# Routed experts in three passes, two of them among the steps of a delta rule

## The chip, the cores and the metric

The kernel runs on one core of a Trainium2 chip. The metric is the time of one execution in microseconds on the device. The engines of the core are PE (matrix products), ACT (scalar engine), DVE (vector engine), POOL (GpSimd) and SP, which only issues transfers. Each runs its own queue of instructions in order and waits on semaphores of the others.

## What is computed

A delta rule with 4 x 8 heads, 768 tokens and head size 48 gives 3072 rows of 384 numbers. A router then sends each row to two of eight experts, and each expert is a two-layer network of 384 to 1024 to 384 numbers. All is float32.

```python
for t in range(S):
    y[:, :, t] = einsum('bhd,bhde->bhe', q[:, :, t], state)
    v_old = einsum('bhde,bhd->bhe', state, k_n[:, :, t])
    state = state + beta[t] * einsum('bhd,bhe->bhde', k_n[:, :, t], v[:, :, t] - v_old)
...
noisy = x @ w_gate + log1p(exp(x @ w_noise)) * noise     # x: 3072 rows of 384
top2, top2_w = two largest of noisy, softmax of the two
for e in range(8):
    rows = tokens with e among their two
    out[rows] += top2_w * (relu(x[rows] @ w1[e]) @ w2[e])
```

A token has two rows, one for each of its experts. Of 6144 rows an expert gets between 711 and 807.

## The kernel before

**Two stages.** The first stage computes the delta rule and the routing, the second the experts.

**First stage.** The 768 tokens are cut into 12 chunks of 64, and two chunks make a step: there are six steps (s = 0 to 5, called steps 1 to 6 in the text), each with four units (two chunks by two pairs of the batch). For each step: `products` transposes k and multiplies it with itself (L433, L449), and copies the diagonal blocks into `gd`; `invert` inverts 32 x 32 triangles on DVE (L495 takes `gd` into `t`, L538 scales by `low_d`, which POOL makes in L531, then thirty columns in L546 and L550, L562 scales, L570 and L576 transpose back to `tb` and `tt`); `within` multiplies q with k (L433, L449, L641); `join` puts the 32-blocks together to 64-blocks `w64` (L594, L606); `recur` carries the state from chunk to chunk (L449 with `st`, L679, L689, L707, L719, and L732 on POOL, which makes `wide`); `answer` gives the rows y and the router's logits (L751, L762, L771, L776); `route` picks the two experts of each token, counts the rows that each expert has so far (`before`; L882 to L888 on PE) and writes each row, with its token number and weights, into the expert's part of the array `rows_x` in DRAM, by eight indirect writes from POOL (L319, called spreads).

**Who sets the order.** In the first stage no loop order is kept. Every piece is a job of the class `Jobs` with an engine, an assumed cost, what it reads and writes, and sometimes a due time (multiples of PACE = 42). `order` places the jobs by these costs, engine by engine, the earliest due first among those that could start at about the same time, and PSUM is given out to the jobs as halves of four pairs of banks. The jobs are then emitted in that order, and each engine's queue is in that order from then on. q, k, v and other operands lie in rings of buffers; a ring's size says how far ahead of its use a load or a product can be made:

```python
NK, NT_, NW = 3 * US, 3 * US - NU, US + NU        # US = 4 units of a step, NU = 2
NQ, N_U, N_ST = 2 * NU, 2 * NU + 1, 3
```

`kps` (k) has NK = 12 slots, `kTs` (its transposes) and `ats` NT_ = 10, `w64s` 6, `us` 5, the states 3.

**Transfers ahead.** While the first steps run, SP also writes empty rows into `rows_x` (eight transfers), clears `out` (one), and loads the weights of the first expert into `w_even`.

**Second stage.** When all rows are written, the eight experts follow one after the other, each with 832 rows: six tiles of 128 and one of 64. For each: the rows are loaded (L1119, L1122), then the weights of the next expert (L285, L286, two buffers of both weights, `w_even` and `w_odd`), the sums so far of these tokens are gathered from `out` (L1084, seven indirect reads on POOL), the rows are transposed (L1023, L1027), the first layer is made in two halves of 416 columns (L1033, ReLU in L1037), the second layer tile by tile (L1058; the tile of 64 in L1044), each result is added to the gathered sum with its weight (L1062, L1049) and scattered back to `out` (L1093). The gathers of an expert wait for the scatters of the one before, since a token has rows of two experts. If an expert had more than 832 rows, a block behind the end would do the rest; with these inputs it is not entered.

The buffers of the second stage lie where the first stage had its own, so they can be written only when that pool's users are done.

Of the kernel before, what the change touches and what calls it, by code (L numbers as in the profile page):

```python
# [21 lines left out]
ROWS = TILES * 128 + MORE  # L22
ROW = 384 + 4
HALF = ROWS // 2

# [3 lines left out]
class Bank:  # L29
# [5 lines left out]
    def __init__(self, size, ahead=False):  # L35
        self.size, self.ahead, self.tile, self.users = size, ahead, None, []


class Jobs:

# [12 lines left out]
    def add(self, engine, cost, emit, reads=(), writes=(), opens=None, uses=None, closes=None,  # L53
            lands=0.0, due=None):
        job = SimpleNamespace(
            engine=engine, cost=cost, emit=emit, opens=opens, closes=closes, lands=lands,
            due=1e9 if due is None else due, after=set(), number=len(self.jobs),
        )
        bank = opens or uses or closes
        if bank:  # L60

            if bank.users:
                job.after.add(bank.users[0])
            if closes:
                job.after.update(bank.users)
            if uses and engine == self.PE:
                job.after.update(bank.users)
            bank.users.append(job.number)
        for key in reads:
            job.after.update(self.wrote.get(key, ()))  # L70
        for key in writes:
            job.after.update(self.wrote.get(key, ()))
            job.after.update(self.read.get(key, ()))
        for key in reads:
            self.read.setdefault(key, []).append(job.number)
        for key in writes:
            self.wrote[key], self.read[key] = [job.number], []
        job.after.discard(job.number)
        self.jobs.append(job)

    def order(self):
        jobs = self.jobs
        for job in reversed(jobs):
            for i in job.after:
                jobs[i].due = min(jobs[i].due, job.due - job.cost - self.SIGNAL)
        waits = [len(job.after) for job in jobs]
# [12 lines left out]
        def place(size, ahead):  # L99

            best = None
            for i, pair in enumerate(halves[: self.AHEAD] if ahead else halves):
                if size == 2:
                    if None not in pair:
                        best = min(best or (1e9,), (max(pair), 0, i, 0))
                    continue
                for z in range(2):
                    if pair[z] is not None:

                        best = min(best or (1e9,), (pair[z], pair[1 - z] is not None, i, z))  # L110
            return best

        done = []
        while len(done) < len(jobs):
            first = {(x, y): place(x, y) for x in (1, 2) for y in (False, True)}
            best = None
            for engine in self.ENGINES:
                at = []
                for i in could[engine]:
                    start = max(free[engine], ready[i])  # L120
                    if jobs[i].opens:
                        room = first[jobs[i].opens.size, jobs[i].opens.ahead]
                        if room is None:
                            continue
                        start = max(start, room[0])
                    at.append((start, jobs[i].due, i))
                if at:
                    soon = min(at)[0] + self.PATIENCE
                    pick = min((x for x in at if x[0] <= soon), key=lambda x: x[1:])
                    best = min(best or (1e9,), pick)  # L130
# [4 lines left out]
            if job.opens:  # L135
                _, _, x, z = first[job.opens.size, job.opens.ahead]
                job.opens.at = x, z
                for y in range(z, z + job.opens.size):
                    halves[x][y] = None
                pair = self.pairs[x]  # L140
                job.opens.tile = pair if job.opens.size == 2 else pair[:, z]
# [17 lines left out]
    AHEAD = 3  # L159
# [6 lines left out]
def kernel(  # L166
# [12 lines left out]
):  # L179

# [101 lines left out]
    def load_weights(pool, e):  # L282
        w1e = pool.tile([128, KT, F], FP32, name="w1e")
        w2e = pool.tile([128, FT, DM], FP32, name="w2e")
        nc.sync.dma_start(out=w1e, in_=w1r[e])  # L285
        nc.sync.dma_start(out=w2e, in_=w2r[e])  # L286
        return w1e, w2e
# [42 lines left out]

    def deltanet(ictx):
# [5 lines left out]
        PE, ACT, DVE, POOL, SP = Jobs.ENGINES  # L337

# [22 lines left out]
        NK, NT_, NW = 3 * US, 3 * US - NU, US + NU  # L361

        NQ, N_U, N_ST = 2 * NU, 2 * NU + 1, 3
        kps = ring([128, H, DP], "kp", NK, lambda t: [t[:, :, D:DP]])
        qps = ring([128, H, DP], "qp", NQ, lambda t: [t[:, :, D:DP]], nc.vector)
# [42 lines left out]
        def load(n, name):  # L408
            c, u = divmod(n, NU)
            src, t, size = {"k": (k, kps, NK), "q": (q, qps, NQ), "v": (v, vs, NQ)}[name]  # L410
# [15 lines left out]
        def turned(n, name, src, size, to, to_size):  # L426

            p = Bank(1, True)
# [26 lines left out]
        def products(n):  # L455
# [6 lines left out]
            p = Bank(2, True)  # L462
# [117 lines left out]
        def join(n):  # L580
# [5 lines left out]
            p = Bank(1)  # L586
# [41 lines left out]
        def within(n):  # L628

            turned(n, "q", qps, NQ, qTs, NQ)  # L630
            p = Bank(2, True)
# [16 lines left out]
        def recur(n):  # L648
# [18 lines left out]
            if c:  # L667
                p_b = Bank(2)
# [15 lines left out]
            p_u = Bank(1)  # L684
# [16 lines left out]
            p_s = Bank(2)  # L701
# [37 lines left out]
        def answer(n):  # L739
# [4 lines left out]
            p_y, p_xt = Bank(1), Bank(1)  # L744
# [76 lines left out]
        def route(s):  # L821
# [8 lines left out]
            p = Bank(1)  # L830
# [115 lines left out]
            for i in range(US):  # L946
                for to in slot:
# [3 lines left out]
                        lands=2.5, due=(s + 1 + (s + 1 < NS)) * PACE,  # L951
                    )

# [5 lines left out]
        held = {}  # L959
        for e in range(E):  # L960
# [6 lines left out]
        jobs.add(  # L967
            SP, 2.0, lambda: held.update(w=load_weights(w_even, 0)), due=3 * PACE
        )

# [8 lines left out]
        jobs.add(SP, 0.7, clear_out, due=4 * PACE)  # L979
        for s in range(NS):  # L980
# [15 lines left out]
            route(s)  # L996
        with tc.manual_schedule(
# [6 lines left out]
        return held["w"]  # L1004

    with ExitStack() as ictx:
        weights = deltanet(ictx)
# [31 lines left out]
    def second_half(w2e, hT, gate, got):  # L1039

        p_o = ps([128, DM], "p_o")
        halves = [slice(lo, lo + MORE) for lo in (0, 64)]
        for fo in range(FT):
            nc.tensor.matmul(  # L1044
                p_o[halves[fo % 2]], hT[:, fo, ROWS - MORE : ROWS], w2e[:, fo],
# [20 lines left out]
    def gates_of(xr, e, gate):  # L1066

        nc.vector.scalar_tensor_tensor(
            out=gate, in0=xr[:, :, DM + 3], scalar=float(e - E), in1=xr[:, :, DM + 2],
            op0=ALU.is_equal, op1=ALU.mult,  # L1070
        )
        nc.vector.tensor_tensor(out=gate, in0=gate, in1=xr[:, :, DM + 1], op=ALU.add)

    def ordered(d, group, earlier):

        tc.declare_no_dep(d, group=group, reason="no token has two rows of an expert")
        tc.add_to_no_dep_group(group, d)
        for i in earlier:
            tc.add_manual_dep(d, i.name, SYNC, reason="sums so far of the same tokens")
        return d  # L1080

    def gather(got, index, group, earlier):
        return ordered(
            nc.gpsimd.indirect_dma_start(  # L1084
                out=got, out_offset=None, in_=out,
                in_offset=bass.IndirectOffsetOnAxis(ap=index, axis=0),
                bounds_check=N - 1, oob_is_err=False,
            ).ins, group, earlier,
        )

    def scatter(got, index, group, earlier):
        return ordered(
            nc.gpsimd.indirect_dma_start(  # L1093
                out=out, out_offset=bass.IndirectOffsetOnAxis(ap=index, axis=0), in_=got,
                in_offset=None, bounds_check=N - 1, oob_is_err=False,
            ).ins, group, earlier,
        )

# [10 lines left out]
    sums = [moe.tile([128, TILES + 1, DM], FP32, name=f"sums{i}", bufs=1) for i in range(2)]  # L1109
    for got in sums:  # L1110
        nc.gpsimd.memset(got, 0.0)
    rows_in = [128] * TILES + [MORE]
    for e in range(E):
        w1e, w2e = weights
        rows = slice(e * N, e * N + TILES * 128)
        more = slice(rows.stop, rows.stop + MORE)
        xr = moe.tile([128, TILES + 1, ROW], FP32, name="xr")
        loads = [
            nc.sync.dma_start(  # L1119
                out=xr[:, 0:TILES], in_=rows_x[rows].rearrange("(t p) d -> p t d", p=128)  # L1120
            ).ins,
            nc.sync.dma_start(out=xr[0:MORE, TILES], in_=rows_x[more]).ins,  # L1122
# [4 lines left out]
        if e + 1 < E:  # L1127
            weights = load_weights(w_odd if e % 2 == 0 else w_even, e + 1)
        index = moe.tile([128, TILES + 1], I32, name="index")
        gate = moe.tile([128, TILES + 1], FP32, name="gate")  # L1130
        for p, t in ((128, slice(0, TILES)), (MORE, slice(TILES, TILES + 1))):
# [4 lines left out]
            gather(got[0:p, i], index[0:p, i : i + 1], f"out{e}", added)  # L1136
# [3 lines left out]
        xe = moe.tile([128, KT, ROWS], FP32, name="xe")  # L1140
        for i, p in enumerate(rows_in):
            transposed(xr, xe, i, p)
        hT = moe.tile([128, FT, ROWS], FP32, name="hT", bufs=1)
        for h0 in range(0, ROWS, HALF):
            first(w1e, xe, hT, slice(h0, h0 + HALF))
        for i, p in enumerate(rows_in):
            if p < 128:
                second_half(w2e, hT, gate[:, i : i + 1], got[:, i])
            else:
                second(w2e, hT, i, gate[:, i : i + 1], got[:, i])  # L1150
            added.append(
                scatter(got[0:p, i], index[0:p, i : i + 1], f"out{e}", gathers if i == 0 else [])
# [79 lines left out]
```

## Time and profile before

| | |
|---|---|
| time, median of 3 runs | 1005.68 us (1004.72 to 1006.64) |
| time of the profiled execution | 1009.23 us |
| its span, first to last instruction | 1007.5 us |
| PE busy | 854.3 us (85%), 8670 matmul records |
| DVE, ACT, POOL busy | 341.5, 250.0, 235.8 us |
| moved by DMA | 95.55 MB, 95 GB/s over the span |
| mean granted TensorE clock | 0.862 of full speed |

A float32 matmul leaves two records in the profile, a transpose one. Records overlap in the array, so the time that one adds is the group's busy time over its count, and its own duration is longer. "Idle before" in a group or a timeline is how long the engine had nothing to run ahead of the instruction, and what ended that. A slice of the page is a fortieth of the span, 25.2 us. The granted clock is the share of full speed that the chip allowed to TensorE.

### The profile page before, as it was taken

Reading aid. Unit: us, or ns where it says so; the run is one execution under the profiler, and the core shown is the slowest. Engines: PE = TensorE matmul, PEld = TensorE weight load, DVE = VectorE, ACT = ScalarE, POOL = GpSimd, SP = SyncE. Lnnn points to the kernel's source line nnn. Section 1 sums busy time; section 2 is a strip of 40 time slices with the busy share of each in tenths; the row PEclk is TensorE's granted clock in tenths of the full one; section 3 lists DMA queues with packets and bytes.
Section 4 is the critical chain, followed back from the end, with each engine's and each line's share of the span. In section 5 each row is a group of like instructions: output and inputs, shape, how many; then the busy total and the mean of one; then the engine's idle time right before and its main releaser. Section 6 shows DMA issues by size and latency. Waiting matters only on the chain. (4 is left out here: it accounts for less than half of the span.)

```text
span 1007.5 us, 20278 instructions
## 1 busy us (share of the span) xinstructions
PE 854.3 (85%) x8670; PEld 581.5 (58%) x8670; DVE 341.5 (34%) x941; ACT 250.0 (25%) x613; POOL 235.8 (23%) x280
## 2 busy tenths in 40 slices
PE   4368778676968767199999999999999999999995
PEld 3267677576857656155555555555555555555552
DVE  6957768496785832210200200201201102002001
ACT  4354635545464243011020020020110110210200
POOL 3120341504315130520121121211301302202111
PEclk7757667596875858599999999999999999999998
DMA  4699631413213010462232412412511521301100
GB/s 79 122 361 374 149 82 26 112 27 89 58 25 96 12 65 3 153 233 74 71 123 79 141 53 87 163 29 88 177 62 40 167 71 54 97 16 42 41 25 28
DMA packets 119765, 95.55 MB, mean 95 GB/s; under 512 B 84558, under 2 KB 109676, under 8 KB 119664
## 3 DMA queue, kind: packets, MB, share of 16 engines
q1 hardware_dynamic: 107568, 65.34, 22.5%
q0 software_dynamic: 9984, 28.42, 8.3%
q8 instruction: 70, 1.15, 0.5%
q10 hardware_dynamic: 2112, 0.39, 0.2%
q14 instruction: 31, 0.25, 0.1%
HBM read 60.10 MB, written 35.60 MB: 95 GB/s over the span
## 5 line engine op out<-in xcount | busy, mean ns | idle before, releaser
L1033 PE MATMUL p_h<-xe,w1e 128*128 128x416 f32 x768 | 271.0, 514 | 6.3 <-DVE xe L1027 6.3
L1058 PE MATMUL p_o<-w2e,hT 128*128 128x384 f32 x768 | 249.0, 486 | 0.0
L1033 PEld LDWEIGHTS p_h<-xe,w1e 128*128 128x128 f32 x768 | 145.6, 190 | 127.5 <-issue 119.9
L1058 PEld LDWEIGHTS p_o<-w2e,hT 128*128 128x128 f32 x768 | 145.9, 190 | 102.2 <-issue 2.5
L1037 ACT ACTIVATE hT<-p_h 128x416 f32<-128x416 f32 x128 | 66.2, 517 | 491.5 <-PE p_h L1033 474.3
L1062 DVE SCALAR_TENSOR_TENSOR sums<-p_o,gate,sums 128x384 f32<-128x384 f32 x48 | 29.7, 618 | 451.9 <-PE p_o L1058 451.9
L1093 POOL DMA_INDIRECT out_dram<-sums,index x56 | 55.1, 983 | 406.3 <-DVE sums L1062 383.9
L1084 POOL DMA_INDIRECT sums<-out_dram,index x56 | 56.0, 999 | 55.5 <-issue 39.7
L546 DVE TENSOR_TENSOR part<-t 128x30 f32<-128x30 f32 (+9 forms) x180 | 63.9, 355 | 5.3
L550 DVE TENSOR_TENSOR t<-t,part 128x30 f32<-128x30 f32 (+9 forms) x180 | 63.1, 350 | 6.2
L319 POOL DMA_INDIRECT rows_x<-y,slot x48 | 47.9, 999 | 56.6 <-DVE r_count L910 29.5
L689 PE MATMUL pair<-v,w 64*64 64x48 f32 x768 | 43.0, 270 | 13.8 <-issue 13.2
L689 PEld LDWEIGHTS pair<-v,w 64*64 64x64 f32 x768 | 39.1, 184 | 16.8 <-issue 16.2
L732 POOL COPY wide<-st 64x384 f32<-64x384 f32 x44 | 29.0, 659 | 63.1 <-DVE st L719 57.4
L620 ACT COPY w<-tt 32x256 f32<-32x256 f32 x96 | 38.6, 402 | 1.8
L1023 PE MATMUL p_xt<-ident,xr 128*128 128x128 f32 (+1 forms) x168 | 22.2, 288 | 17.6 <-DMA xr<-rows_x 17.6
L449 PE MATMUL pair<-qT,kT 64*64 64x64 f32 x768 | 21.3, 269 | 17.9 <-DVE qk L641 9.0
L478 ACT COPY gd<-pair 32x256 f32<-32x256 f32 x88 | 31.9, 362 | 17.2 <-PE pair L449 14.2
L558 POOL MEMSET t<- 128x32 f32 x6 | 0.9, 156 | 139.5 <-DVE t L550 139.5
L1023 PEld LDWEIGHTS p_xt<-ident,xr 128*128 128x128 f32 (+1 forms) x168 | 19.5, 151 | 23.4 <-issue 23.4
L606 PE MATMUL pair<-w,x 32*32 32x32 f32 x768 | 25.2, 229 | 8.8 <-ACT x L601 3.3
L449 PE MATMUL pair<-kT 64*64 64x64 f32 x768 | 20.4, 273 | 13.4 <-ACT kT L438 7.6
(134 smaller groups left out, 830.5 us busy)
## 6 DMA issues: line engine op xcount, KB each, us to landing
w1e<-in_moe_w_dram SPq DMA_DIRECT2D x8, 1536.0 KB
w2e<-in_moe_w_dram SPq DMA_DIRECT2D x8, 1536.0 KB
rows_x<-empty SPq DMA_DIRECT2D x8, 1358.0 KB
xr<-rows_x SPq DMA_DIRECT2D x8, 1164.0 KB
v<-in_v_dram SPq DMA_DIRECT2D x48, 96.0 KB
qp<-in_q_dram SPq DMA_DIRECT2D x48, 96.0 KB
out_dram<-empty SPq DMA_DIRECT2D x1, 4608.0 KB
kp<-in_k_dram SPq DMA_DIRECT2D x44, 96.0 KB
```

Of the source, the lines that this page charges most:

```text
L319: d = nc.gpsimd.indirect_dma_start(out=rows_x, out_offset=bass.IndirectOffsetOnAxis(ap=slot, axis=0), in_=rows, in_offset=None,).ins
L449: nc.tensor.matmul(out[rows_of[b], z, j], lhsT[rows_of[z], j, rows_of[b]], rhs(rows_of[z], j, b), start=(j == 0), stop=(j == NP - 1), skip ...
L546: v_.tensor_tensor(out=part, in0=t_inv[:, j + 1 :, j, None].to_broadcast(shape), in1=t_inv[:, None, j, 0:j].to_broadcast(shape), op=ALU.mult,)
L550: v_.tensor_tensor(out=t_inv[:, j + 1 :, 0:j], in0=t_inv[:, j + 1 :, 0:j], in1=part, op=ALU.add)
L620: lambda rows=rows, cols=cols: nc.scalar.copy(w64[rows, :, cols], tt[rows]),
L689: nc.tensor.matmul(per_head(p_u)[b, h], w64[b, h], v_n[b, h], start=(h == 0), stop=(h == H - 1), skip_group_check=True,)
L1023: nc.tensor.transpose(p_xt[:, do, 0:rows], xr[0:rows, i, do * 128 : (do + 1) * 128], ident[0:rows, 0:rows],)
L1033: nc.tensor.matmul(p_h, w1e[:, do, fo * 128 : (fo + 1) * 128], xe[:, do, cols], start=(do == 0), stop=(do == KT - 1),)
L1037: nc.scalar.activation(hT[:, fo, cols], p_h, ACTF.Relu)
L1058: nc.tensor.matmul(p_o, hT[:, fo, i * 128 : (i + 1) * 128], w2e[:, fo], start=(fo == 0), stop=(fo == FT - 1),)
L1084: nc.gpsimd.indirect_dma_start(out=got, out_offset=None, in_=out, in_offset=bass.IndirectOffsetOnAxis(ap=index, axis=0), bounds_check=N - ...
L1093: nc.gpsimd.indirect_dma_start(out=out, out_offset=bass.IndirectOffsetOnAxis(ap=index, axis=0), in_=got, in_offset=None, bounds_check=N - ...
```

## The change

The experts are done in three passes. The first pass takes the first two tiles (256 rows) of each expert once step 2 is routed, the second the next two once step 4 is routed, and the third the remaining 2 x 128 + 64 rows at the end. To make the cut fit, an expert that has fewer than 256 (or 512) rows by then has its count raised to that, so that its later rows begin behind the cut (`cut`); the rows left out stay empty ones. By these inputs no expert ends above 807 rows.

The sixteen turns of the first two passes (`work_on`: one expert, two tiles) are jobs of the planner of the first stage, marked `late`: among jobs that could start at about the same time a late one comes behind all others, and late ones follow each other by turn. They use PSUM pair 0 alone, which from step 3 on the delta rule leaves to them, one buffer for each of the two weights, which are loaded once in each pass, and two buffers for rows, gathered sums and transposed rows. To make room, rings of the delta rule become smaller: `kps` 8 slots, `kTs` and `ats` 8, `w64s` 5, q 3, `us` 4, the states 2. In the last pass the first layer of an expert is made in one piece of 320 columns. Clearing `out` is due earlier.

```diff
+CUT = 2
+PASSES = 2
+LAST = TILES - PASSES * CUT
...
+        for job in jobs:
+            job.key = (0, job.due) if job.late is None else (1, job.late)
...
-                    at.append((start, jobs[i].due, i))
+                    at.append((start, jobs[i].key, i))
...
+        def bank(s, size, ahead=False):
+            among = (0, 1, 2, 3) if s < 2 else (1, 2, 3)
+            return Bank(size, among[:-1] if ahead else among)
...
-        NK, NT_, NW = 3 * US, 3 * US - NU, US + NU
-        NQ, N_U, N_ST = 2 * NU, 2 * NU + 1, 3
+        NK, NT_, NW = 2 * US, 2 * US, US + 1
+        NQ, NQ_IN, N_U, N_ST = 2 * NU, 3, 2 * NU, 2
...
+        def cut(rows):
+            p = Bank(1, (1, 2, 3))
+            missing = sb([1, E], f"missing{rows}")
+            def skip():
+                nc.vector.tensor_scalar(
+                    out=missing, in0=p.tile[0:1, 0:E], scalar1=-1.0, scalar2=float(rows),
+                    op0=ALU.mult, op1=ALU.add,
+                )
+                nc.vector.scalar_tensor_tensor(
+                    out=before[0:1], in0=missing, scalar=0.0, in1=before[0:1],
+                    op0=ALU.max, op1=ALU.add,
+                )
+            jobs.add(PE, 0.4, lambda: nc.tensor.matmul(p.tile[:, 0:E], ones, before),
+                     reads=["before"], opens=p)
+            jobs.add(DVE, 0.4, skip, writes=["before"], closes=p)
+
+        def work_on(x, e, steps):
+            turn = x * E + e
+            z = turn % 2
+            r0 = e * N + x * CUT * 128
+            xr, got, xe, index, gate = xrs(z), gots(z), xes(z), indices[z], gates(z)
+            tiles = range(CUT)
...
+            jobs.add(SP, 0.7, lambda: nc.sync.dma_start(out=w1e, in_=w1r[e]),
+                     writes=["w1"], lands=8.0, late=turn - 0.7)
+            jobs.add(SP, 0.7, lambda: nc.sync.dma_start(out=w2e, in_=w2r[e]),
+                     writes=["w2"], lands=8.0, late=turn - 0.4)
+            jobs.add(
+                SP, 0.7, load_rows,
+                reads=[("rows", s, i, y) for s in steps for i in range(US) for y in (0, 1)],
+                writes=[("xr", z)], lands=2.5, late=turn - 0.9,
+            )
+            jobs.add(DVE, 0.6, of_rows, reads=[("xr", z)], writes=[("gate", z)], late=turn - 0.8)
+            for i in tiles:
+                jobs.add(
+                    POOL, 1.3,
+                    lambda i=i: added_by.setdefault((turn, "got"), []).append(
+                        gather(got[:, i], index[:, i : i + 1], f"out{turn}", added_by[turn - 1])
+                    ),
+                    reads=[("gate", z), *(("out", turn - 1, j) for j in tiles)],
+                    writes=[("got", z, i)], lands=2.5, late=turn - 0.1,
+                )
...
+            for fo in range(FT):
+                p = Bank(1, (0,))
+                def hidden(fo=fo, p=p):
+                    for do in range(KT):
+                        nc.tensor.matmul(
+                            p.tile[:, 0 : CUT * 128], w1e[:, do, fo * 128 : (fo + 1) * 128],
+                            xe[:, do], start=(do == 0), stop=(do == KT - 1),
+                        )
+                jobs.add(
+                    PE, 1.3, hidden, reads=["w1", *(("xe", z, i) for i in tiles)], opens=p,
+                    late=turn,
+                )
...
+            for i in tiles:
+                p = Bank(1, (0,))
+                for f0 in range(0, FT, 2):
+                    def back(i=i, p=p, f0=f0):
+                        for fo in range(f0, f0 + 2):
+                            nc.tensor.matmul(
+                                p.tile[:, 0:DM], hT[:, fo, i * 128 : (i + 1) * 128],
+                                w2e[:, fo], start=(fo == 0), stop=(fo == FT - 1),
+                                skip_group_check=True,
+                            )
+                    jobs.add(
+                        PE, 1.3, back,
+                        reads=["w2", *(("hT", fo) for fo in range(FT))], late=turn + 0.5,
+                        **({"uses": p} if f0 else {"opens": p}),
+                    )
+                jobs.add(
+                    DVE, 0.65,
+                    lambda i=i, p=p: nc.vector.scalar_tensor_tensor(
+                        out=got[:, i], in0=p.tile[:, 0:DM], scalar=gate[:, i : i + 1],
+                        in1=got[:, i], op0=ALU.mult, op1=ALU.add,
+                    ),
+                    reads=[("gate", z)], writes=[("got", z, i)], closes=p, late=turn + 0.5,
+                )
...
-        jobs.add(
-            SP, 2.0, lambda: held.update(w=load_weights(w_even, 0)), due=3 * PACE
-        )
...
             route(s)
+            if s % 2 and s + 1 < NS:
+                x = s // 2
+                cut((x + 1) * CUT * 128)
+                for e in range(E):
+                    work_on(x, e, range(2 * x, 2 * x + 2))
...
+    both = room_for_weights(w_odd), weights_even
     for e in range(E):
-        w1e, w2e = weights
-        rows = slice(e * N, e * N + TILES * 128)
+        w1e, w2e = both[e % 2]
+        nc.sync.dma_start(out=w1e, in_=w1r[e])
+        r0 = e * N + PASSES * CUT * 128
+        rows = slice(r0, r0 + LAST * 128)
...
-        for h0 in range(0, ROWS, HALF):
-            first(w1e, xe, hT, slice(h0, h0 + HALF))
+        first(w1e, xe, hT, slice(0, LAST * 128 + MORE))
```

## The prediction

> **What bounds the kernel now.** I read the span in slices first, then the busy times of three stretches, then the costliest groups, then the timelines of the two places where the stretches meet the change. The slices show two kernels in one:
>
> ```profile
> PE   4368778676968767199999999999999999999995
> DVE  6957768496785832210200200201201102002001
> PEclk7757667596875858599999999999999999999998
> ```
>
> The first 16 slices are the delta rule, in which no engine is full and the granted TensorE clock moves between half and full. From slice 17 on PE is full at full clock: the experts. The same by stretches (PE, PEld, DVE, ACT, POOL busy, then granted clock, DMA share, GB/s):
>
> ```profile
> 176.00:405.00 229.00, 170.44 (x4178) 152.85 (x4171) 143.34 (x404) 102.42 (x274) 68.95 (x82) 0.72 0.21 54
> 405.00:431.00 26.00, 6.51 (x30) 5.93 (x30) 5.92 (x25) 0.00 (x0) 15.36 (x14) 0.50 0.55 190
> 431.00:997.00 566.00, 557.70 (x1813) 315.47 (x1811) 66.09 (x157) 66.18 (x128) 107.57 (x110) 1.00 0.26 85
> ```
>
> So PE idles 59 us in steps 3 to 6 of the delta rule, then nearly all of a 24.6 us hand-over (406.5, end of the last routing matmul, to 431.05), and 8 us in the experts. What an expert matmul costs is in the groups, as busy time over count, since matmuls overlap: 271.0/768 = 0.353 us for a record of 416 columns (0.848 ns a column) and 249.0/768 = 0.324 us for 384. Each float32 matmul leaves two records.
>
> ```profile
> L1033 PE MATMUL p_h<-xe,w1e 128*128 128x416 f32 x768 | 271.0, 514 | 6.3 <-DVE xe L1027 6.3
> L1058 PE MATMUL p_o<-w2e,hT 128*128 128x384 f32 x768 | 249.0, 486 | 0.0
> ```
>
> What paces the delta rule is the inversion on DVE, one per step, with one buffer t:
>
> ```profile
> 237.13 1.93 DVE L495 STREAM_TRANSPOSE t<-gd 128x1024 f32<-128x1024 f32 x1
> 253.87 0.56 DVE L719 TENSOR_TENSOR st<-pair,st 128x384 f32<-128x384 f32 x1 [7.92 <-PE pair L707]
> 256.44 1.22 DVE L538 TENSOR_TENSOR t<-t,low_d 128x1024 f32<-128x1024 f32 x1
> 289.83 1.22 DVE L562 TENSOR_TENSOR low_d<-t,d 128x1024 f32<-128x1024 f32 x1
> 296.61 1.87 DVE L495 STREAM_TRANSPOSE t<-gd 128x1024 f32<-128x1024 f32 x1
> ```
>
> It begins (L495), waits for the state update in the queue ahead of it (L719, 7.92 us for PE), multiplies (L538), runs its columns (to L562) and the next begins at once: 59.5 us from L495 to L495. The L562 instants of steps 2 to 6 are 106.6, 166.4, 229.9, 289.8 and 350.5; the last routing matmul starts at 404.1. PE pieces between a routing and L538 are on this chain, pieces between L538 and the next routing lie beside DVE's columns. The hand-over:
>
> ```profile
> 417.02 0.96 POOL L319 DMA_INDIRECT rows_x<-y,slot  x1 [0.30 <-issue]
> 420.18 0.37 SPq L1119 DMA_DIRECT2D xr<-rows_x  x1
> 426.53 4.58 PE L1023 MATMUL p_xt<-ident,xr 128*128 128x128 f32 x21 [17.65 <-DMA xr<-rows_x]
> 431.05 34.51 PE L1033 MATMUL p_h<-xe,w1e 128*128 128x416 f32 x96
> ```
>
> Eight spreads at 1.27 us, landing, the load of the rows, transposes; PE has nothing else to do.
>
> **The change: what moves.** A turn (two tiles of an expert) has 24 first-layer matmuls of 256 columns (48 x 256 x 0.848 ns = 10.4 us), 16 second-layer ones (32 x 0.324 = 10.4) and 6 transposes (0.126 each, from 16.1 us for 129). In the built program's order on PE only 72 of the 384 first-layer matmuls, 40 of the 256 second-layer ones and 24 of the 96 transposes stand ahead of the last routing: 31.3 + 25.9 + 3.0 = 60.2 us. Three turns of 16 are among the delta rule; 13 first layers and 13.5 second layers follow it in one block. The total of columns is the old one (256 + 256 + 320 = 832), as is the count of gathers and scatters (56 each). New are 32 weight loads of 1.5 MB.
>
> **Sum behind the delta rule.** Routing matmuls 2.4. The block: 13 x 10.4 + 13.5 x 10.4 = 275.6, and 13 turn boundaries. There the last ReLU (between 0.362, a copy of 256 columns, and 0.517, the ReLU of 416), the second transpose and the copy of the first one stand in a row ahead of the second layer, because the block has only two half pairs of PSUM: about 1.15 us a turn with its 0.76 of transposes, 15 in all (bounds 0.76 and 2.5: 10 to 33). Weights have one buffer: the next first-layer load may start when the first layer is done and has 11.5 us, the other has 10.4. The stretch 424 to 442 moved 339 to 376 GB/s, so 1.57 MB is 4.2 to 4.7 us and 2.3 to land (927.2 to 929.3, a scatter's): 7 us, hidden with 3 to spare; with the cover gone, each us late costs 13. Scatter, landing, two gathers (0.92 + 2.2 + 2 x 1.3 + 2.2, rows at 926 to 932) end 8 us into a turn whose sums are wanted at 16: hidden. Block: 291.
>
> Then a second hand-over: the first tail load waits for all readers of the delta pool, that is for the last scatter: sum 0.9, scatter 1.3, landing 2.3, then a weight load and the rows 6.5 and a transpose and copy 2: 13 us (bounds 0, were nothing waited for, and the 24.6 of now). The tail: 48 x 320 x 0.848 = 13.0, 32 x 0.324 = 10.4, half tile 2.7 (496.45 to 499.18), nine transposes and their copy 2.4: 28.5 an expert, 228. From the last matmul to the end 10.5, as now (997.0 to 1007.5).
>
> Sum: 404.1 + 2.4 + 291 + 13 + 228 + 10.5 = 949, plus what the delta rule stretches, x. The old hand-over is gone because the block fills it, and the 60.2 us left the back.
>
> **What the delta rule stretches.** Rings shrink (k 12 to 8 slots, its transposes 10 to 8, PSUM pairs 4 to 3 from step 3 on), and the order changes with them: the products of the next step (L449), on which L495 waits, no longer stand ahead of the routing but within the join. I place L495 by the PE rows ahead of it, then 10 us to L538 (transpose 1.9, squares 0.4, ACT root 2.5, lengths 2, low_d on POOL 2.34), then 32 us to L562: columns 127.0/6 = 21.2 and their gaps 2, L538 itself 1.2, routing 5.4, rest 2 (it is 33.4 to 43 now, with waits that then lie ahead of L538).
> Step 2: L495 behind the state update at 124 (now 112.5), L562 at 169.7: +3.
> Step 3: DVE takes indices and gates of the first two turns ahead of the state update and L495, and PE their transposes ahead of L707. They wait for the eight spreads (now issued to 190.1, then to about 188.5, and 2.2 to land) and a row load (3): L495 at 200 (now 175.4). POOL holds low_d behind two gathers; queued with it are wide and v, and the answers of the step wait for these. L562 at 241: +11.
> Step 4: the second-layer pieces (10.4) and five first-layer ones (6.5) stand between the routing and L707; the two sums on DVE stand ahead of L495, a scatter, its landing and two gathers on POOL ahead of low_d. L495 about 25 us behind the routing, now 8; the 7.92 wait is gone in exchange. L562 at 303: +13.
> Step 5: 10.4 us of second layer, but half of it while DVE makes tb and tt: L562 at 361, +10.5. Step 6: pieces of 3.9 and 5.2 lie in the waits for tb and for the routing's logits: last routing at +12.
> On SP three weight loads stand ahead of q and v loads of steps 5 and 6; 4.2 to 4.7 us each, 0 to 9 on the path: 3. So x = 15. Bounds: 60, nothing hidden; -5, if dense PE work raises the clock: rows of 32 records take 1.06 to 1.14 at 0.50 clock and 0.69 at full, a dozen ahead of each L538, 5 us a step.
>
> In 250 to 260 us the granted clock is 0.50 though PE reads 8.84 of 10 busy, so a piece may well start at half clock; I price the pieces at full clock, because they make the stretch denser, and leave the rest to the bound of 60. [...]
>
> **Total.** 949 + 15 = 964 of span. The profiled execution of now has a span of 1007.5 and a time of 1009.2, 3.5 above the median of the runs, so I expect 962.
>
> **Rivals.** (a) The chain through DVE loses all pieces and the reordering: L495 a further 10 us late in four steps, on top of 60: 949 + 100 = 1049 at worst, 1020 in the middle. For it: two queues, DVE and POOL, now wait for expert data ahead of the inversion. Against: 59 us of PE idleness, and L538 waits for PE already. It decides from 59 us, some 15 a step. Slower, 0.13. (b) The block is bound by its loads: late by 4 us a turn, 962 + 52 = 1014; for it the single buffers, against it 4.1 MB a turn is 190 GB/s where 376 was moved. 0.07. (c) The clock goes up among the pieces and x is -5 or less: 935 to 942. For it the 0.72 clock, against it DVE's columns, which no clock shortens. 0.09. (d) The parts cancel: 0.03.
>
> **Numbers.** Forecast 962, chance 0.68, itself from 942 to 1000. With (c) faster is 0.77 and some more from (a) and (b) when they cost half: 0.79; within 0.2% (about what these runs can tell from no change) 0.03; slower 0.18. The range 938 to 1003 leaves out a fifth.
>
> **What would show it.** L562 instants near 170, 241, 303, 361; the last routing near 419; a block of 13 turns of 22 us with PE full; 13 us without PE near 715; eight experts of 28.5. Wrong would be turns over 24 us (loads), L562 intervals over 75 us (a), or under 58 throughout (c).

## The result, and the profile after

The changed kernel is slower: 1166.29 us in the median (1161.95 to 1166.67, four runs) against 1006.16, a ratio of 1.158 (95% interval 1.154 to 1.162). The prediction was 962. The span of the profiled execution is 1164.2 us, 200 more than the 964 that the sum gave. The span in slices, first PE's busy tenths, then the granted clock:

```profile
PE   4574693698786887977777777877775799999995
PEclk7566585599897995999999999999999899999998
```

Slices 18 to 30 are the block of turns behind the last routing. There the clock is full and yet PE is busy only seven or eight tenths of the time. In the kernel before, everything behind the hand-over read nine. The block takes 404 us (488.9 to 893.3) where 291 were forecast. Two turns' edge in PE's timeline (start, duration, engine, line; in brackets the idle time before and what ended it), then the ReLUs of the same moment on ACT:

```profile
616.97 1.46 PE L1093 MATMUL pair<-xe,w1e 128*128 128x256 f32 x6
619.14 1.56 PE L1093 MATMUL pair<-xe,w1e 128*128 128x256 f32 x6 [0.71 <-DVE got L1128]
621.22 1.56 PE L1093 MATMUL pair<-xe,w1e 128*128 128x256 f32 x6 [0.52 <-ACT hT L1104]
623.32 1.56 PE L1093 MATMUL pair<-xe,w1e 128*128 128x256 f32 x6 [0.53 <-ACT hT L1104]
```

```profile
620.78 0.38 ACT L1104 ACTIVATE hT<-pair 128x256 f32<-128x256 f32 x1 [14.04 <-PE pair L1093]
622.88 0.38 ACT L1104 ACTIVATE hT<-pair 128x256 f32<-128x256 f32 x1 [1.71 <-PE pair L1093]
```

The first piece of the turn ends at 618.43, but its ReLU starts only at 620.78, 0.08 us after the second piece has ended (619.14 + 1.56); and the third piece starts 0.06 us after that ReLU. PE and ACT take turns although two banks are there: a piece every 2.10 us, where its six records of 256 columns need 1.30. A turn lasts 30.86 us (602.94 to 633.80, from transpose to transpose), not 22. PE's three longest sums of waits in the block, by what it waited for (total us, times, longest):

```profile
PE pair L1093 <- ACT hT L1104: 40.7, 77, 0.5
PE pair L1077 <- ACT xe L1082: 10.8, 12, 0.9
PE pair L1115 <- DVE got L1128: 10.0, 13, 0.8
```

No transfer is among them, nor among the six smaller sums (24.4 us together, at most 0.8 each time): the weight loads are hidden, as forecast.

The other loss lies in the delta rule. The last L938 (the count of earlier rows, L888 before) runs at 488.5 instead of 405.9, 82.7 us late, where 15 were forecast. DVE's timeline shows the form of it:

```profile
190.88 1.21 DVE L612 TENSOR_TENSOR low_d<-t,d 128x1024 f32<-128x1024 f32 x1
236.38 1.98 DVE L545 STREAM_TRANSPOSE t<-gd 128x1024 f32<-128x1024 f32 x1 [1.66 <-ACT gd L528]
244.73 1.26 DVE L588 TENSOR_TENSOR t<-t,low_d 128x1024 f32<-128x1024 f32 x1
275.86 1.22 DVE L612 TENSOR_TENSOR low_d<-t,d 128x1024 f32<-128x1024 f32 x1
310.77 1.95 DVE L545 STREAM_TRANSPOSE t<-gd 128x1024 f32<-128x1024 f32 x1 [0.51 <-ACT gd L528]
```

From L588 to L612, the inversion itself, it is 31 to 35 us in steps 3 to 6, a few less than the 33 to 43 before. But the next inversion (L545) now begins 35 to 46 us behind the last one's end, where it began 6 to 9 behind. So a step takes 76 to 85 us from L612 to L612 (67 in step 2) instead of 60. The first such gap (36.3 us, from 114.1 to 150.4) opens in step 2, long before the first expert matmul at 234.7.

The rest is near the forecast or small: PE is idle 14.1 us ahead of the tail (13 forecast), a tail expert takes 30.6 us (28.5), and 13.5 us follow the last matmul (10.5).

### The profile page after: what moved, and what is told of

Read it like the earlier page. It is cut to its first block, busy times and chain, and to the rows that moved or that the text cites. A ratio compares the mean times of both kernels' runs of the same rounds, so it can differ in the third digit from the quotient of the medians.

```text
span 1164.2 us, 21352 instructions
## 1 busy us (share of the span) xinstructions
PE 901.4 (77%) x9058; PEld 630.2 (54%) x9058; DVE 333.3 (29%) x958; ACT 274.4 (24%) x709; POOL 237.0 (20%) x278
## 5 line engine op out<-in xcount | busy, mean ns | idle before, releaser
L1093 PE MATMUL pair<-xe,w1e 128*128 128x256 f32 x768 | 199.1, 396 | 54.9 <-ACT hT L1104 44.8
L1115 PE MATMUL pair<-w2e,hT 128*128 128x384 f32 x512 | 184.3, 507 | 19.4 <-DVE got L1128 10.0
L1093 PEld LDWEIGHTS pair<-xe,w1e 128*128 128x128 f32 x768 | 138.0, 191 | 111.9 <-ACT hT L1104 78.3
L1115 PEld LDWEIGHTS pair<-w2e,hT 128*128 128x128 f32 x512 | 95.1, 194 | 91.6 <-DVE got L1128 18.1
L1104 ACT ACTIVATE hT<-pair 128x256 f32<-128x256 f32 x128 | 48.7, 383 | 346.9 <-PE pair L1093 334.9
L1228 PE MATMUL p_h<-xe,w1e 128*128 128x320 f32 x384 | 117.3, 470 | 11.3 <-DVE xe L1222 11.3
L1228 PEld LDWEIGHTS p_h<-xe,w1e 128*128 128x128 f32 x384 | 78.9, 207 | 46.8 <-DVE xe L1222 12.5
L1254 PE MATMUL p_o<-w2e,hT 128*128 128x384 f32 x256 | 83.9, 486 | 0.0
L1254 PEld LDWEIGHTS p_o<-w2e,hT 128*128 128x128 f32 x256 | 48.6, 190 | 33.1
L360 POOL DMA_INDIRECT got<-out_dram,index x32 | 32.9, 1028 | 92.8 <-DMA out_dram<-got,index 72.9
```

The costliest lines, as they stand in the source:

```text
L360: nc.gpsimd.indirect_dma_start(out=got, out_offset=None, in_=out, in_offset=bass.IndirectOffsetOnAxis(ap=index, axis=0), bounds_check=N - ...
L1093: nc.tensor.matmul(p.tile[:, 0 : CUT * 128], w1e[:, do, fo * 128 : (fo + 1) * 128], xe[:, do], start=(do == 0), stop=(do == KT - 1),)
L1104: lambda fo=fo, p=p: nc.scalar.activation(hT[:, fo], p.tile[:, 0 : CUT * 128], ACTF.Relu),
L1115: nc.tensor.matmul(p.tile[:, 0:DM], hT[:, fo, i * 128 : (i + 1) * 128], w2e[:, fo], start=(fo == 0), stop=(fo == FT - 1), skip_group_check ...
L1228: nc.tensor.matmul(p_h, w1e[:, do, fo * 128 : (fo + 1) * 128], xe[:, do, cols], start=(do == 0), stop=(do == KT - 1),)
L1254: nc.tensor.matmul(p_o, hT[:, fo, i * 128 : (i + 1) * 128], w2e[:, fo], start=(fo == 0), stop=(fo == FT - 1),)
```

## The experiments

They ran on three chips (0, 11 and 12 on record), on each of which the kernel before takes 988 us and not 1006, so ratios are compared. They are called the second chip here, and the one of the result the first; its number is not on record, and that it is another is taken from the 1006 us. The changed kernel itself ran on the first only. The times in the first four expectations are on the first chip's scale. One run took the kernel before along for its trace.

> The kernel before once more, for its trace beside the next three runs (the earlier batch ran it in 987.67 us where the first profile took 1009.23). Both theories: the experts take the same 603 us from the last routing to the end, and the difference to 1009 lies in the delta rule, so its last routing stands at 404 less that difference.

It took 988.35 us, with the last L888 at 385.7: the 20 us between the chips lie ahead of it, and 601 us follow it on both (986.6 - 385.7 and 1007.5 - 405.9). "Late" below is against 385.7, and against 405.9 on the first chip.

**The rings alone, and the k rings alone.** In the kernel before:

```
-        NK, NT_, NW = 3 * US, 3 * US - NU, US + NU
-        NQ, N_U, N_ST = 2 * NU, 2 * NU + 1, 3
+        NK, NT_, NW = 2 * US, 2 * US, US + 1
+        NQ, NQ_IN, N_U, N_ST = 2 * NU, 3, 2 * NU, 2
...
```

The second run changes the first of these lines alone and keeps NW at US + NU.

> The kernel before with nothing but the smaller rings of the change (k 12 to 8 slots, its transposes and their masked products 10 to 8, w64 6 to 5, q 4 to 3, u 5 to 4, st 3 to 2); no expert is moved, four PSUM pairs. Theory A: the 84 us by which the last routing came late (487.8 against 404.1 us) are the rings, since the first lags arise in steps 2 and 3 (114.1 against 106.6 and 190.9 against 166.4 us), before any expert matmul runs (the first at 234.7). Then the last routing is at 465 to 485 and the time 1065 to 1085 us. Theory B: the expert pieces and the waits they bring stretch steps 4 to 6, and the rings cost only the 7.5 to 24 us seen up to step 3: 1015 to 1030 us.

Measured 1018.53 us, ratio 1.031 (1.022 to 1.040), last L888 29.0 us late. This meets neither theory: the rings cost a third of the 83 us.

> As the run before, but only the rings of k (12 to 8) and of its transposes and products (10 to 8) are cut; w64, q, u and st keep their sizes. Theory A1: the products of the next step can no longer be made while the present one recurs, so these rings make all of the ring loss: within 10 us of the run with all rings cut. Theory A2: the others (u, st, q, w64) hold the recurrence up: under half of its loss.

Measured 1036.22, ratio 1.049 (1.040 to 1.057), 48.1 late. Neither A1 nor A2: cutting less costs more. A step takes one of two forms: the next inversion begins either 5 to 13 us behind the last or 28 to 46 behind it. With all rings cut one step fell into the long gap, with k's alone three did. In these long gaps, and in those of the changed kernel, L545 starts 2.3 to 3.3 us after the last of the step's four products (L449 before, L499 after the change) has started, so a step takes the long form when one of these stands late on PE. Where it stands is the planner's order, and that came out differently in these two runs although the second cuts less.

**Two tiles instead of one for the experts' two banks.** In the changed kernel:

```
...
-        jobs = Jobs([psum.tile([128, 2, 512], FP32, name=f"pair{i}") for i in range(4)])
+        two = [psum.tile([128, 512], FP32, name=f"half{z}") for z in range(2)]
+        jobs = Jobs([two] + [psum.tile([128, 2, 512], FP32, name=f"pair{i}") for i in (1, 2, 3)])
...
-            among = (0, 1, 2, 3) if s < 2 else (1, 2, 3)
+            among = (0, 1, 2, 3) if s < 2 and size == 1 else (1, 2, 3)
```

> The changed kernel with the experts' PSUM pair allotted as two tiles of one bank each instead of one tile of two banks (pairs of two banks are then taken from the other three in every step). Theory C: the 0.53 us for which PE waits after each first-layer piece come from ReLU and matmul waiting for each other across the two banks of one tile (ReLU of piece n begins 0.08 us after the end of piece n+1), and two tiles part them: a turn falls from 30.85 to 22 to 23 us, 13.5 turns behind the delta rule give back 105 to 120 us: 1045 to 1062 us. Theory D: two banks are too few for a piece of 1.56 us and a ReLU of 0.38 us whatever the tiles: turns stay at 30 to 31 us and the time at 1155 to 1170.

Measured 996.27 us, ratio 1.008 (1.006 to 1.011): 15 points of the 15.8 are gone, by an edit that changes only how PSUM is handed out. PE in one turn of the block, then the ReLUs beside it:

```profile
467.31 10.52 PE L1096 MATMUL half<-xe,w1e 128*128 128x256 f32 x48
477.67 0.49 PE L1080 MATMUL half<-ident,xr 128*128 128x128 f32 x3
478.37 0.55 PE L1080 MATMUL half<-ident,xr 128*128 128x128 f32 x3 [0.21 <-ACT hT L1107]
478.76 10.57 PE L1118 MATMUL half<-w2e,hT 128*128 128x384 f32 x32
```

```profile
468.81 0.38 ACT L1107 ACTIVATE hT<-half 128x256 f32<-128x256 f32 x1 [11.23 <-PE half L1096]
470.10 0.38 ACT L1107 ACTIVATE hT<-half 128x256 f32<-128x256 f32 x1 [0.91 <-PE half L1096]
```

Each ReLU now starts when its own piece is done, every 1.30 us, and PE runs through. A turn is 21.86 us (467.31 to 489.17): theory C, and theory D falls. It holds in every run: from the third turn of the block on, a turn is 30.8 to 30.9 us in the three kernels with one tile and 21.8 to 22.2 in the five with two. The rest of the gain lies in the delta rule: the last count is 44.6 us late instead of 82.7, with three long gaps instead of four. What shortened that is not parted: two-bank jobs no longer use this pair in steps 1 and 2, and the order is another.

**All experts behind the delta rule.** In the changed kernel the turns are added after the last step, and their transposes and first-layer pieces read the running counts:

```
-                jobs.add(PE, 0.4, turned_rows, reads=[("xr", z)], opens=p, late=turn - 0.6)
+                jobs.add(PE, 0.4, turned_rows, reads=[("xr", z), "before"], opens=p, late=turn - 0.6)
...
```

> The changed kernel with all sixteen turns held back until the last routing has been counted (transposes and first-layer pieces also read the running counts); nothing of an expert is left on PE in the delta rule. Rings, cuts and tail as in the change. Theory A (rings): the last routing stays late, at 465 to 485 us, and with 2.5 more turns of 30.85 in the block the time is 1215 to 1250 us. Theory B (pieces): the last routing comes back to 411 to 430 us, the block still grows by 77 us: 1165 to 1185.

Measured 1222.09 us, ratio 1.237 (1.226 to 1.247), the last count at 464.5: 78.8 us late without one expert matmul ahead of it. Theory B falls. Of the experts' other work only two turns' row loads and gates with one turn's gathers (203.7 to 212.3 us), one load of both weights and the two cuts (207.8 and 364.4) are left ahead of the last count, and two of the four long gaps (112.7 to 143.2 and 262.5 to 298.7) have none of it beside them. But the rings alone gave 29.0. The other 50 may be the PSUM pair that is kept from the delta rule, alone or with the rings, or one more turn of the planner's order.

**The pair alone.**

> The kernel before with its rings whole, but from step 3 on one of its four PSUM pairs is left unused, as in the change; no expert is moved. The run with all experts behind was 80 us late at the last routing without one expert matmul ahead of it, and the rings alone cost 31. Theory G: the pair costs the other 50: ratio 1.04 to 1.06. Theory E: with the k slots there, three pairs are enough: ratio 0.998 to 1.012, and rings and pair cost 80 only together.

Measured 985.90 us, ratio 0.998 (0.996 to 0.999), last count 0.4 us late. Three pairs are enough as long as the rings are whole, so theory G falls. How much of the 79 us the pair adds to small rings is not parted: the k rings alone cost 48.1 with all four pairs, and the run with two tiles, which has the same rings and keeps the same pair back from step 3 on, is 44.6 late.

**Ten k slots.** In the changed kernel, one number:

```
-        NK, NT_, NW = 2 * US, 2 * US, US + 1
+        NK, NT_, NW = 2 * US + NU, 2 * US, US + 1
```

> The changed kernel with one number changed: the ring of k has 10 slots instead of 8 (before: 12); all else, the one-tile PSUM pair among it, as in the change. Theory E: a k slot is free only when the state update of its old unit (L757) is done, and those of the second half of a step are the last jobs ahead of the routing, so with 8 slots the k loads and products of the next step miss the gap beside the inversion and wait until the join is over (28 to 45 us from L612 to L545 instead of 6 to 12). With 10 slots they do not: L545 follows L612 within 15 us in most steps, the last routing comes 40 to 60 us earlier than in the change, the ratio to before falls from 1.158 to 1.10 to 1.12. Theory F: the other rings, the pair given up or the pieces on PE hold the step up: the ratio stays above 1.14.

The last count is 12.9 us late instead of 82.7. DVE's timeline:

```profile
172.56 1.22 DVE L612 TENSOR_TENSOR low_d<-t,d 128x1024 f32<-128x1024 f32 x1
179.27 1.91 DVE L545 STREAM_TRANSPOSE t<-gd 128x1024 f32<-128x1024 f32 x1
223.38 1.22 DVE L612 TENSOR_TENSOR low_d<-t,d 128x1024 f32<-128x1024 f32 x1
234.26 1.96 DVE L545 STREAM_TRANSPOSE t<-gd 128x1024 f32<-128x1024 f32 x1 [0.18 <-ACT gd L528]
```

The gaps are 6.7 and 10.9 us, in all later steps at most 11.0: theory E, for the delta rule. The last of a step's four products, 33 to 43 us behind L612 in the changed kernel, is at most 8.1 us behind it here. For the whole it was too hopeful: 1122.14 us, ratio 1.136 (1.133 to 1.139), 21 us for 70. A shorter delta rule holds fewer pieces. By the built order 23.6 us of expert matmuls stand ahead of the last routing, not 60.2, and the missing 36.6 went into turns of 30.86 us instead of 21.9, which is 52.

How the k slots do it can be read in the changed kernel's trace around 170 us. PE's state updates, the k loads on SP, then PE's products for the next inversion and the copies that give their PSUM pair back:

```profile
169.16 0.68 PE L757 MATMUL pair<-u,kp 64*64 64x48 f32 x32
171.21 0.68 PE L757 MATMUL pair<-u,kp 64*64 64x48 f32 x32
...
196.29 1.13 PE L499 MATMUL pair<-kT 64*64 64x64 f32 x32 [4.18 <-DVE st L769]
223.72 1.10 PE L499 MATMUL pair<-kT 64*64 64x64 f32 x32
229.27 1.10 PE L499 MATMUL pair<-kT 64*64 64x64 f32 x32
...
233.89 0.90 PE L499 MATMUL pair<-kT 64*64 64x64 f32 x32
```

```profile
169.88 3.34 SPq L466 DMA_DIRECT2D kp<-in_k_dram  x4
```

```profile
222.80 0.37 ACT L534 COPY at<-pair 128x256 f32<-128x256 f32 x1
228.22 0.38 ACT L534 COPY at<-pair 128x256 f32<-128x256 f32 x1
```

The k load leaves 0.04 us after the state update that frees its slot, shortly before the routing (184.4). The first product comes only at 196.29, when a pair is free, and the next at 223.72, after the copy L534 at 222.80 has given the pair back; on ACT that copy stood behind those of the join. The fourth starts at 233.89 and L545 at 236.38. In the kernel before, three of the four products of this step ran at 160.8, ahead of the routing. That the copy's place costs so much is read from this trace; that 10 slots mend it was run.

**Both repairs.**

> Both repairs: two PSUM tiles for the experts and 10 k slots. If theories C and E hold and their parts add, the run with two tiles (ratio 1.008) loses a further 35 to 50 us: ratio 0.95 to 0.975, which would beat the kernel before. If E fails: 0.99 to 1.01.

990.23 us, ratio 1.003 (1.001 to 1.006). The parts did not add. The last count comes 28.8 us earlier than with two tiles alone (401.5 against 430.3), but with 23.6 us of matmuls ahead of it instead of 51.7, and the 28 us come back behind it.

**The second hand-over.** With both repairs, the turns' tiles and banks get pools of their own, opened ahead of the delta rule's:

```
+    turns = ctx.enter_context(tc.tile_pool(name="turns", bufs=1))
+    psum_e = ctx.enter_context(tc.tile_pool(name="psum_e", bufs=1, space=bass.MemoryType.PSUM))
...
-        tc.tile_pool(name="psum", bufs=8, space=bass.MemoryType.PSUM)
+        tc.tile_pool(name="psum", bufs=6, space=bass.MemoryType.PSUM)
```

> Two PSUM tiles and 10 k slots as in the run before it (ratio 1.003), and now the turns' tiles (rows, sums, transposed rows, hidden layer, and the two PSUM banks) lie in pools opened ahead of the delta rule's and kept to the end, so that the delta rule's room is free when its own last spread has read it and not after the last turn's scatter. Theory H: the 14.2 us without PE ahead of the tail (729.3 to 743.9) are the tail's first weight and row loads waiting for that room; they now land during the turns: gap under 2 us, ratio 0.987 to 0.992. Rival: these loads wait for the last scatter or stand behind others on SP all the same: ratio 1.000 to 1.005.

978.76 us, ratio 0.991 (0.989 to 0.994). The tail's first transposes in the run before, and here the end of the last turn's second layer, behind which the tail goes on:

```profile
742.57 2.02 PE L1221 MATMUL p_xt<-ident,xr 128*128 128x128 f32 x9 [14.14 <-DMA xr<-rows_x]
```

```profile
721.68 10.48 PE L1129 MATMUL half<-w2e,hT 128*128 128x384 f32 x32
732.00 8.78 PE L1242 MATMUL p_h<-xe,w1e 128*128 128x320 f32 x32
```

The 14 us are gone, so they were the wait for room (theory H).

**The tail's transposes ahead.** In addition, the loads and transposes of expert e+1 stand behind the first layer of e:

```
+        first(w1e, xe, hT, slice(0, LAST * 128 + MORE))
+        if e + 1 < E:
+            ahead = prepare(e + 1)
...
```

> As the run before, and in the tail each expert's rows are loaded and transposed behind the first layer of the expert ahead of it, not behind its second one. Theory I: a tail expert takes 28.9 to 30.6 us instead of the 26.3 of its matmuls because PE waits 1.55 us for the copy of the transposed rows each time, and in some of them runs the first matmuls after that wait at half clock (1.7 us); both go: 12 to 17 us off, ratio 0.970 to 0.978. Rival: the copies then hold up the second layer or its banks: the same as the run before.

961.91 us, ratio 0.975 (0.972 to 0.977): faster than both kernels. A tail expert takes 27.36 us (757.17 to 784.53). The same edit in the kernel before shows what of this has nothing to do with the change:

> The kernel before, with nothing but the transposes of the next expert put behind the first layer of the present one. It shows how much of the gain of such a tail has nothing to do with the change. Its experts wait 0.90 us each for the copy: 6 us off, ratio 0.992 to 0.996. Rival: the transposes lie in the same place on PE and nothing else is shorter: 0.998 to 1.002.

983.33 us, ratio 0.996 (0.994 to 0.997), so half a point of the 2.5.

**The same without work in the delta rule.** In the run with the transposes ahead, all turns are put behind the last count, by the edits of the run with all experts behind.

> As the run before, but no expert work at all is put among the delta rule: all sixteen turns follow the last routing. What is left of the change is that turns on the rows of the first four steps fill the wait for the last rows. The run with 10 slots and two tiles moved 23.6 us of matmuls ahead of the last routing and had it 15.8 us later than the kernel before (401.5 against 385.7). If these prices hold, this run's routing is back at 385 to 390 and it is 6 to 10 us slower than the run before: ratio 0.977 to 0.987. Rival: the pieces in the delta rule bring nothing: same or faster than the run before.

989.28 us, ratio 1.002 (1.000 to 1.004), 27 us slower than with the pieces, where 6 to 10 were expected. The last count stands at 401.8 us without a single piece ahead of it and at 402.0 with 23.6 us of them. From 176 us to the last count, without pieces and with them (busy times of PE, PEld, DVE, ACT, POOL, then granted clock, DMA share, GB/s):

```profile
176.00:402.00 226.00, 179.75 (x4340) 162.16 (x4335) 151.90 (x418) 106.81 (x284) 69.53 (x87) 0.70 0.25 64
```

```profile
176.00:402.00 226.00, 192.60 (x4429) 169.08 (x4423) 151.98 (x420) 111.34 (x297) 72.34 (x89) 0.78 0.29 76
```

The pieces cost nothing where they lie. PE's own busy time grows by only 12.9 us, and the granted clock rises from 0.70 to 0.78: the matmuls around the pieces take that much less. The 16 us by which both are late belong to the rest of the change (rings, pair, cuts, the first turns' loads), which no run parts further; my price for the pieces, taken from that lateness, was wrong.

## Why the prediction was wrong

- **"the block has only two half pairs of PSUM: about 1.15 us a turn"** is the step that failed worst. The working saw the scarce banks, but charged a wait only at the edge between the layers (bounds 10 to 33 us for the block) and let ReLU and matmul overlap within a layer. They did not, since the two banks are one tile. Measured 30.86 against the 21.95 a turn that the working gives, 8.9 more, on some 13 turns: 113 us of the 200. With two tiles the turn is 21.86, so the sum of its other terms was right.
- **x = 15** was 82.7, beyond its bound of 60: 68 us of the 200. The working named the cause, that "the products of the next step" come later, and then placed L545 too early: at 124 in step 2 (150.4 measured) and 200 in step 3 (236.4). It weighed each ring and the pair as small shifts; the runs show jumps, a gap of 28 to 46 us between two inversions instead of 5 to 13. Small rings bring them (one with all rings cut, 29 us late; three with k's alone, 48), the pair alone brings none (0.4), rings and pair together bring three or four (45 and 79), and two k slots take them away (12.9).
- **The pieces' own cost**, on which the range and rivals (a) and (c) were built, was the wrong question. Three turns among the delta rule is what the order held (60.2 us), but at no price, as the runs at 401.8 and 402.0 show for 23.6 us of them; with all 60.2 the last count is 82.7 us late, without any 78.8, on two chips. Rival (a) had the delta rule late, for a reason that the 78.8 us without any piece exclude as the main one. Two of the prediction's own signs of being wrong came, but with another cause than it named: turns over 24 us (not from loads) and intervals over 75 us between the inversions' ends (not from rival (a)).
- **The clock.** The prediction held that a piece may start at half clock, and priced all pieces at full clock. Measured in the changed kernel, the granted clock over the 224 records of pieces ahead of the last count is 0.94 in the mean, and 21 of them ran at half clock from start to end.
- **The second hand-over**, 13 against 14.1, and its reason were right, as was the weight loads' being hidden (rival b).
- **The tail expert**, 28.5 against 30.6: its transposes and their copy were 2.75 instead of 2.4, and 1.7 us is a half-clock start, told below (seven of the eight have one). With 1 us of the hand-over and 3 at the end this is the remaining 19 us.

## What to carry to other kernels

Two buffers are double buffering only if what tracks dependences sees two (here 30.86 us a turn with one tile, 21.86 with two). When a piece's consumer starts right after the next piece's end, look at how the banks are allotted before looking at the engines. In a pipeline ordered by a planner, the room taken for new work can cost more than the work (here 78.8 us without a piece among the delta rule, and nothing for 23.6 us of pieces): price each ring by the event that frees its slot and by what that event now misses, and expect jumps rather than slopes (here gaps of 5 to 13 us or of 28 to 46). And a loss that shows up together with the moved work is not yet caused by it; the run that keeps the room and leaves the work out tells.

## What was not expected of the hardware

In the tail of the changed kernel seven experts wait 1.55 us for the copy of their transposed rows, and six of them then start their first layer at half clock. One such start, with the transposes and the wait ahead of it, and the same place in the last expert, which does not (us of the stretch, busy times of PE, PEld, DVE, ACT, POOL, granted clock, DMA share, GB/s):

```profile
1029.93:1032.68 2.75, 1.20 (x11) 0.90 (x9) 2.57 (x7) 0.00 (x0) 0.63 (x1) 1.00 0.66 143
1032.68:1033.15 0.47, 0.47 (x2) 0.39 (x3) 0.27 (x4) 0.00 (x0) 0.29 (x1) 1.00 0.97 350
1033.17:1036.56 3.39, 3.39 (x8) 2.14 (x7) 0.00 (x0) 0.44 (x1) 0.00 (x0) 0.50 1.06 388
1036.59:1040.00 3.41, 3.41 (x14) 2.42 (x13) 0.22 (x2) 0.87 (x2) 1.44 (x2) 1.00 0.27 91
...
1126.00:1128.00 2.00, 2.00 (x9) 1.45 (x8) 0.00 (x0) 0.44 (x1) 1.04 (x1) 1.00 0.00 0
```

About 3.4 us run at half speed and cost 1.7 (14.88 us for a first layer instead of 13.19). It is not the wait alone, as the last expert shows, nor the load at the same time: with both repairs (second chip) seven experts waited 1.55 us, the first of them beside such a load (issued at 773.89), and none slowed down (13.19 us each); in the run that took the second hand-over away the first five did and the last two did not.

In this tail the granted clock is 0.50 for 3.41 us each from 941.00, 971.72, 1002.44, 1033.16, 1063.88 and 1094.60 us, so the drops are 30.72 us apart. The experts follow each other at 30.61 us, the 1.7 lost us included, so each first layer starts 0.11 us farther ahead of its drop than the one before: 0.15, 0.26, 0.37, 0.48, 0.58 and 0.70 us. The last first layer, from 1124.52 to 1137.71, has the full clock throughout. What brings the drops, and why this last one escapes, is not shown. Without the wait (the run with transposes ahead) all seven later experts take 13.19.

The two chips differ by 20 us on the same program, all of it in the delta rule, and agree within 1 us on the 601 us of experts. Up to 166 us the two traces agree within 0.3 us; from then on each stretch from one L562 to the next, and from the last one to the last count, is 4 to 6 us shorter on the second. PE in the second of these stretches, on the first chip (some of its rows) and then the same 64 records on the second:

```profile
243.26 1.95 PE L689 MATMUL pair<-v,w 64*64 64x48 f32 x25
...
247.71 0.37 PE L689 MATMUL pair<-v,w 64*64 64x48 f32 x3 [0.98 <-issue]
...
250.59 1.53 PE L689 MATMUL pair<-v,w 64*64 64x48 f32 x24 [0.98 <-issue]
```

```profile
239.49 3.65 PE L689 MATMUL pair<-v,w 64*64 64x48 f32 x64
```

On the first chip PE stops in the middle of equal matmuls, for nothing that the profile shows ("issue"), and the 64 records take 8.86 us (243.26 to 252.12) instead of 3.65. From 20 us to the last count there are 39 such stops of 26.4 us together, on the second chip four of 7.8; the changed kernel, also on the first, has 39 of 25.0, and no experiment has more than 11 (15.7 us). They are on the path at least in part: the wait for the state update that the prediction read as 7.92 us is 2.7 on the second chip. Why PE stops there stays open.
